# Rotary attention and a sigmoid-gated MLP in one kernel: weights decoded in fewer bit operations, and keys rotated together with queries

## The chip, the cores and the metric

The program runs on one core of one Trainium2 chip. Its engines are TensorE (PE, with its weight loads as PEld), VectorE (DVE), ScalarE (ACT) and GpSimd (POOL); SyncE (SP) issues the transfers. The metric is device microseconds of one execution; three runs of the kernel before have a median of 735.48 us (735.28 to 738.73).

## The reference

Four batches of eight heads, 576 positions, head size 64. Keys and queries are rotated (rotary embedding), attention is a softmax over 576 keys, and its output goes through a gated MLP (512 to 1536 to 512). The three MLP weights reach the kernel as 64-bit floats.

```python
def rotate(x):
    x1, x2 = (x[..., :half], x[..., half:])
    return np.concatenate([x1 * cos - x2 * sin, x1 * sin + x2 * cos], axis=-1)
scores = np.matmul(rotate(q), rotate(k).transpose(0, 1, 3, 2)) / np.sqrt(64)
attn = softmax(scores)
x = np.matmul(attn, v)             # (4, 8, 576, 64) -> (2304, 512)
out = (sigmoid(x @ w_gate) * (x @ w_val)) @ w_out
```

## The kernel before

**Order.** The program is written as tasks with a rank, a modelled cost, and tokens that they read and write. `Plan.order()` is a list scheduler: it takes the costs and ranks and gives each engine one fixed order, which is then emitted. SP's transfers are tasks in it too. So a changed cost moves instructions on every engine, and each engine and SP's queue run strictly in the order emitted.

**Work.** A batch's attention runs over four head pairs and two halves of the queries (256 and 320 columns). A half of a pair is two or three query blocks (128, 128, and a last one of 64 rows for both heads). Per block and head: scores on PE (line 470 for the first two batches, in f32), a scaled copy with row minimum on DVE (505), Exp on ACT (510), sum and reciprocal on DVE (513, 515), a scaled f16 copy on ACT (275) and its remainder on DVE (281). SP then transposes the block into `pt` (537); for the 64-row block it first moves the second head's rows next to the first's (`p<-p`, 534). The product with the values is on PE (547, tile `pv`), evicted into `xt` by ACT (275) and DVE (281). After the four pairs of a half, a small chain finds a scale: DVE reductions (556, 562), PE (252), DVE (254), PE (257), DVE (239 to 243, tile `c_s`). The MLP follows per half: `m<-xt,w` on PE (598), tanh on ACT (604), gating on DVE (608), split on ACT and DVE (275, 281, tile `gt`), then `m<-wo,gt` on PE (632).

**Weights.** `w_in_chunk` handles 12 chunks of 1024 numbers per partition for gate and value, `w_out_decode` 12 chunks of 512 for the output. Each 64-bit number is two words, `hi` and `lo`. ACT takes the sign from `hi` (286, tanh into int8) and prepares `lo` (291); DVE makes the 32-bit number in three operations (295, 298, 302). Then ACT takes the largest magnitude (324; 354 for `w_out`), PE spreads it (264), and ACT and DVE split the number into two f16 parts (275, 281, tile `w`). Chunks of `w_in` are staged in three slots; those of `w_out` in two, so the transfer of chunk n (348) waits for the DVE operation that last reads chunk n-2.

**Rotation.** `keys_queries` loads keys and queries of a pair side by side (411, x) and the same with swapped halves (412, y, tile `sw`, two buffers). For batches 0 and 1 DVE makes x*cos, y*sin and their sum for keys and for queries apart: six operations of 576 columns (416, 418, 420). For batches 2 and 3 POOL does the same.

Of the kernel before, what the change touches and what calls it, by code (L numbers as in the profile page):

```python
# [10 lines left out]
F32 = mybir.dt.float32  # L11
# [14 lines left out]
TINY = 2.0 ** -100  # L26


W_STEP = 0.5493 / 1.2 * 2.0 ** 15
NW = 2  # L30
TERMS = ((0, 0), (1, 0), (0, 1))
HALVES = ((0, 256), (256, 320))
# [124 lines left out]
def rope_attention_then_sigmoid_glu(ctx: ExitStack, tc: tile.TileContext, qk, v, w_in, w_out, tables, out):  # L157
# [57 lines left out]
    def op(e, us, rank, reads, writes, fn, port=False):  # L215
        P.add(((e, us),), rank, reads, writes, lambda _: fn(eng.get(e)), port=port)

    def op2(us, rank, reads, writes, fn):
        op("DVE", us, rank, reads, writes, fn, port=True)
# [61 lines left out]
        V.scalar_tensor_tensor(out=o, in0=src, scalar=scale, in1=hi, op0=ALU.mult, op1=ALU.subtract)  # L281


    def signs(o, hi):

        A.activation(o, hi.bitcast(F32), AF.Tanh, scale=W_STEP)

    def low_bits(lo):

        w = lo.bitcast(U32)  # L290
        A.activation(w, w, AF.Copy, scale=2.0 ** -29 * (1 - 2.0 ** -12), bias=2.0 ** -9 - 2.0 ** -13 - 0.5)

    def bits_1(o, hi):

        V.tensor_scalar(out=o, in0=hi, scalar1=3, scalar2=0x40000000, op0=ALU.logical_shift_left, op1=ALU.bitwise_xor)  # L295

    def bits_2(o, lo):
        V.scalar_tensor_tensor(out=o, in0=o, scalar=0x7FFFFFFF, in1=lo, op0=ALU.bitwise_and, op1=ALU.bitwise_or)  # L298

    def bits_3(o, sg):  # L300
        r = o.bitcast(F32)
        V.scalar_tensor_tensor(out=r, in0=r, scalar=3e38, in1=sg, op0=ALU.min, op1=ALU.mult)  # L302

    stage = [wo16[:, 4 * n:4 * n + 4].rearrange("p f a c -> p (f a c)").bitcast(I32).rearrange(
        "p (n w) -> p n w", w=2) for n in range(3)]
# [1 line left out]
    def w_in_chunk(f, rank):  # L307
        slot = ring("stage", 3)
        tok = [("wo", 4 * slot + n) for n in range(4)]
        t = stage[slot]  # L310
        hi, lo = t[:, :, 1], t[:, :, 0]
        dst = w16[:, f].rearrange("p g a c n -> p g a (c n)")
        sg = w16[:, f, 1].rearrange("p a c n -> p (a c n)").bitcast(I8)[:, 1024:2048]
        W = ("w", f)
        dma(rank - 0.15, [], tok, 1024, lambda: Y.dma_start(out=t.rearrange("p n w -> p (n w)"), in_=w_in[f].bitcast(I32)))
        op("ACT", c_act(1024), rank, tok, [W], lambda E: signs(sg, hi))
        op("ACT", c_act(1024), rank, [], tok, lambda E: low_bits(lo))
        op2(0.7, rank, [W], tok, lambda E: bits_1(hi, hi))
        op2(c_dve(1024, two=True), rank, [], tok, lambda E: bits_2(hi, lo))
        op2(c_dve(1024, two=True), rank, [W], tok, lambda E: bits_3(hi, sg))  # L320
        r = hi.bitcast(F32).rearrange("p (g n) -> p g n", g=2)
        M = ("wm", f)
        for g in range(2):
            op("ACT", c_act(512) + 0.2, rank, tok, [M, W], lambda E, g=g: A.activation(
                dst[:, g, 0], r[:, g], AF.Abs, accum_out=w_m[:, f, g:g + 1]))
        place = m_place()
        top = allsum(rank, w_m[:, f], 2, place, [M])
        pow2(rank, top, w_s[:, f], w_i[:, f], 14, [place[1]], [("ws", f)])
        for g in range(2):
            op("ACT", c_act(512), rank, tok + [("ws", f)], [W], lambda E, g=g: scaled(  # L330
                A, dst[:, g, 0], r[:, g], w_s[:, f, g:g + 1]))
# [9 lines left out]
    def w_out_decode(f, rank):  # L341
        o, tok = wo_slot(f)
        n = f % 2
        X = ("tmp", n)
        XT = [("xt", 1, p, i) for p in (0, 1) for i in range(2)] if n == 0 else [("xt", 1, p, i) for p in (2, 3) for i in range(2)]
        words = tmp[n][:, 0:1024].rearrange("p (n w) -> p n w", w=2)
        hi, lo, sg = words[:, :, 1], words[:, :, 0], tmp[n][:, 1024:1152].bitcast(I8)
        dma(rank - 0.05, [], [X] + XT, 512, lambda: Y.dma_start(out=tmp[n][:, 0:1024], in_=w_out[f].bitcast(I32)))
        op("ACT", c_act(512), rank, [], [X], lambda E: signs(sg, hi))
        op("ACT", c_act(512), rank, [], [X], lambda E: low_bits(lo))  # L350
        op2(0.4, rank, [X], [tok], lambda E: bits_1(o, hi))
        op2(c_dve(512, two=True), rank, [X], [tok], lambda E: bits_2(o, lo))
        op2(c_dve(512, two=True), rank, [X] + XT, [tok], lambda E: bits_3(o, sg))
        op("ACT", c_act(512) + 0.2, rank, [tok], ["sink", "wob"], lambda E: A.activation(
            sink[:, 0:512], o.bitcast(F32), AF.Abs, accum_out=wo_b[:, f:f + 1]))

# [42 lines left out]
    def keys_queries(b, p, rank):  # L399
# [365 lines left out]
```

## Time and profile before

| | |
|---|---|
| median of 3 runs | 735.48 us |
| span of the profiled execution | 733.1 us (the runs' median lies 2.4 us above it) |
| PE busy | 632.3 us, 86% |
| DVE busy | 526.3 us, 72% |
| ACT busy | 462.8 us, 63% |
| POOL busy | 74.8 us, 10% |
| chain that ended last, by engine | PE 73%, DVE 18%, DMA 4% |

Views used below. The page's slices: 40 equal parts of the span (18.3 us each), a digit is the busy share in tenths. The table by stretches: from:to, length, then busy us (and instructions) of PE, PEld, DVE, ACT and POOL, the granted TensorE clock (1.00 is full), the DMA engines' share, GB/s. The groups: line, engine, operation, out<-in, shape, count | busy us, mean ns of one | idle time of the engine just before and what ended it. The chain: start, length in us, what. The timeline: start, length, engine, line, operation.

### The profile page before, as it was taken

Reading aid. Unit: us, or ns where it says so; the run is one execution under the profiler, and the core shown is the slowest. Engines: PE = TensorE matmul, PEld = TensorE weight load, DVE = VectorE, ACT = ScalarE, POOL = GpSimd, SP = SyncE. Lnnn points to the kernel's source line nnn. Section 1 sums busy time; section 2 is a strip of 40 time slices with the busy share of each in tenths; the row PEclk is TensorE's granted clock in tenths of the full one; section 3 lists DMA queues with packets and bytes.
Section 4 is the critical chain, followed back from the end, with each engine's and each line's share of the span. In section 5 each row is a group of like instructions: output and inputs, shape, how many; then the busy total and the mean of one; then the engine's idle time right before and its main releaser. Section 6 shows DMA issues by size and latency. Waiting matters only on the chain.

```text
span 733.1 us, 12435 instructions
## 1 busy us (share of the span) xinstructions
PE 632.3 (86%) x4642; PEld 414.7 (57%) x4642; DVE 526.3 (72%) x1194; ACT 462.8 (63%) x940; POOL 74.8 (10%) x54
## 2 busy tenths in 40 slices
PE   2355885873279999999999999999999999999997
PEld 1133573551146754577657765578667756866753
DVE  6998899988988973688879998688948574421320
ACT  3767899886556984577758768676757564322320
POOL 0400000000031100014313130131300000000000
PEclk9976697786589999999999999999999999999999
DMA  9965744746934174389596779966483534000001
GB/s 365 318 140 148 233 130 165 198 128 175 255 106 130 34 176 113 86 175 190 130 199 140 160 147 195 202 149 138 105 187 90 118 70 115 1 2 29 1 9 35
DMA packets 187484, 100.55 MB, mean 137 GB/s; under 512 B 171040, under 2 KB 176288, under 8 KB 185376
## 3 DMA queue, kind: packets, MB, share of 16 engines
q1 hardware_dynamic: 187424, 99.77, 54.4%
q8 instruction: 36, 0.59, 0.3%
q14 instruction: 24, 0.20, 0.1%
HBM read 43.12 MB, written 4.72 MB: 65 GB/s over the span
## 4 chain that ended last, share of the span: by engine, by line
PE 73%; DVE 18%; DMA 4%; issue 2%; ACT 2%; SPq 0%; DVEq 0%; ACTq 0%
PE m L598 34%; PE m L632 19%; PE pv L547 9%; PE s L470 5%; PE s L482 5%; DVE p L281 3%; DMA pt<-p 3%; DVE p L505 2%; DVE wo L298 2%; DVE wo L302 2%; DVE sw L418 1%; DVE stk L420 1%; DVE w L281 1%; DMA sw<-in_qk_dram 1%; DVE wo L295 1%
## 5 line engine op out<-in xcount | busy, mean ns | idle before, releaser
L598 PE MATMUL m<-xt,w 128*128 128x320 f16 (+1 forms) x2304 | 303.6, 290 | 8.0 <-ACT w L275 2.6
L598 PEld LDWEIGHTS <-w 128*128 128x128 f16 x2304 | 224.9, 99 | 79.2 <-issue 14.9
L632 PE MATMUL m<-wo,gt 128*128 128x512 f16 x648 | 145.9, 380 | 0.0
L510 ACT ACTIVATE p<-p,st 128x576 f32<-128x576 f32 x144 | 110.6, 769 | 51.8 <-DVE p L505 43.4
L281 DVE SCALAR_TENSOR_TENSOR p<-p,st,p 128x576 f16<-128x576 f32 x144 | 117.2, 845 | 21.9 <-ACT p L275 21.3
L470 PE MATMUL s<-stk 64*128 64x288 f32 (+1 forms) x320 | 70.0, 508 | 52.7 <-DVE p L505 38.2
L275 ACT ACTIVATE p<-p,st 128x576 f16<-128x576 f32 x144 | 104.3, 764 | 14.6 <-DVE st L515 3.5
L632 PEld LDWEIGHTS <-gt 128*128 128x128 f16 x648 | 62.1, 98 | 73.1 <-issue 4.0
L547 PE MATMUL pv<-pt,v 128*64 128x256 f16 (+3 forms) x960 | 77.1, 312 | 21.5 <-DMA pt<-p 21.5
L608 DVE SCALAR_TENSOR_TENSOR th<-th,m 128x256 f32<-128x256 f32 (+1 forms) x96 | 43.1, 450 | 67.7 <-PE m L598 66.1
L275 ACT ACTIVATE gt<-th,c_s 128x256 f16<-128x256 f32 (+1 forms) x96 | 50.3, 528 | 50.0 <-DVE th L608 49.5
L547 PEld LDWEIGHTS <-v 128*64 128x64 f16 (+1 forms) x960 | 54.1, 118 | 44.7 <-issue 29.1
L470 PEld LDWEIGHTS s<-stk 64*128 64x128 f32 (+1 forms) x320 | 35.4, 210 | 76.6 <-DVE p L505 47.5
L604 ACT ACTIVATE th<-m,gsc 128x256 f32<-128x256 f32 (+1 forms) x96 | 47.1, 493 | 36.6 <-PE m L598 35.4
L281 DVE SCALAR_TENSOR_TENSOR gt<-th,c_s,gt 128x256 f16<-128x256 f32 (+1 forms) x96 | 53.4, 562 | 19.1 <-ACT gt L275 19.0
L505 DVE TENSOR_SCALAR_CACHE_REDUCE p<-s,q_e 128x576 f32<-128x576 f32 x72 | 57.5, 812 | 10.6 <-PE s L482 10.0
L505 DVE TENSOR_SCALAR_CACHE_REDUCE p<-s 128x576 f32<-128x576 f32 x72 | 53.4, 751 | 15.0 <-PE s L470 14.5
L418 POOL TENSOR_TENSOR sw<-sw,tab 128x576 f32<-128x576 f32 x16 | 25.4, 1590 | 264.7 <-DVE xm L556 174.1
L482 PE MATMUL s<-stk 128*128 128x288 f16 (+1 forms) x320 | 44.4, 288 | 0.4 <-DVE p L505 0.4
L416 POOL TENSOR_TENSOR qk<-qk,tab 128x576 f32<-128x576 f32 x16 | 25.1, 1593 | 181.0 <-DMA qk<-in_qk_dram 137.5
L275 ACT ACTIVATE o<-m,o_s 128x512 f32<-128x512 f32 x16 | 11.0, 685 | 42.2 <-PE m L632 42.0
L482 PEld LDWEIGHTS <-stk 128*128 128x128 f16 (+1 forms) x320 | 27.4, 100 | 13.9 <-issue 5.4
(94 smaller groups left out, 508.8 us busy)
## 6 DMA issues: line engine op xcount, KB each, us to landing
wo<-in_w_dram SPq DMA_DIRECT2D x12, 1024.0 KB, 5.6
sw<-in_qk_dram SPq DMA_DIRECT2D x16, 576.0 KB, 5.1
xt<-in_wo_dram SPq DMA_DIRECT2D x12, 512.0 KB, 4.4
stk<-in_qk_dram SPq DMA_DIRECT2D x8, 576.0 KB, 4.5
xt<-in_v_dram SPq DMA_DIRECT2D x4, 1152.0 KB, 6.6
qk<-in_qk_dram SPq DMA_DIRECT2D x8, 576.0 KB, 6.0
out_dram<-o SPq DMA_DIRECT2D x16, 256.0 KB, 2.2
stk<-sw SPq DMA_DIRECT2D x16, 216.0 KB, 3.6
```

The costliest lines, as they stand in the source:

```text
L275: A.activation(o, src, AF.Copy, scale=scale)
L281: V.scalar_tensor_tensor(out=o, in0=src, scalar=scale, in1=hi, op0=ALU.mult, op1=ALU.subtract)
L418: either(places, rank, gate, [Z[m]], lambda E, m=m: E.tensor_tensor(out=y[:, m], in0=y[:, m], in1=tab[:, 1], op=ALU.mult))
L470: T.matmul(s_ps[to[e]][hs if width == 64 else slice(0, 128), c, 0:288], lhsT=qT[hs, rows:rows + width], rhs=kT[hs, c * 288:c * 288 + 288], ...
L482: T.matmul(o[:, c, 0:288], lhsT=q[:, rows:rows + width], rhs=kk[:, c * 288:c * 288 + 288], start=(m == 0), stop=(m == 1))
L505: lambda E, h=h, c=c: V.tensor_scalar(out=p32[prs[c]].rearrange("p (c n) -> p c n", c=2), in0=s_ps[h][:, :, 0:288], scalar1=down, scalar2= ...
L510: lambda E, c=c: A.activation(p32[prs[c]], p32[prs[c]], AF.Exp, bias=st[:, k, 0, c:c + 1], scale=-1.0, accum_out=st[:, k, 1, c:c + 1]))
L547: T.matmul(v_ps[64 * e:64 * e + 64, 0:n], lhsT=v16[hs, p, a, g, :], rhs=pt[z][hs, c * 9 + g, 0:n], start=(first and m == 0), stop=(last an ...
L598: T.matmul(m_ps[m][:, 0:n], lhsT=w16[:, f, g, a, cc, :], rhs=x[:, cc, c, c0:c0 + n], start=(k == 0), stop=(k == 11))
L604: op("ACT", c_act(n), rank - 0.05, [("m", m), ("gsc", b, f)], [("th", r)], lambda E, m=m: A.activation(t, m_ps[m][:, 0:n], AF.Tanh, scale= ...
L608: op("DVE", c_dve(n, psum=True), rank - 0.05, [("m", m)], [("th", r)], lambda E, m=m: V.scalar_tensor_tensor(out=t, in0=t, scalar=1.0, in1 ...
L632: T.matmul(m_ps[m], lhsT=gt[:, f, a, c0:c0 + 128], rhs=wo16[:, f, c, :], start=(f == 0 and k == 0), stop=(f == NF - 1 and k == 2))
```

## The change

The weight decode: ACT now multiplies `hi`, read as a 32-bit float, by a power of two in place (a correction of the exponent) instead of taking its sign through tanh into a buffer of its own, and DVE builds the number in two operations, `magnitude` and `signed`, instead of three. The rotation for batches 0 and 1: x*cos, y*sin and the sum are each one operation over keys and queries together (1152 columns; the table is broadcast over the two).

```diff
-    def signs(o, hi):
-        A.activation(o, hi.bitcast(F32), AF.Tanh, scale=W_STEP)
+    def exponents(hi):
+        w = hi.bitcast(F32)
+        A.activation(w, w, AF.Copy, scale=2.0 ** -112)
...
-    def bits_1(o, hi):
-        V.tensor_scalar(out=o, in0=hi, scalar1=3, scalar2=0x40000000, op0=ALU.logical_shift_left, op1=ALU.bitwise_xor)
-    def bits_2(o, lo):
-        V.scalar_tensor_tensor(out=o, in0=o, scalar=0x7FFFFFFF, in1=lo, op0=ALU.bitwise_and, op1=ALU.bitwise_or)
-    def bits_3(o, sg):
-        r = o.bitcast(F32)
-        V.scalar_tensor_tensor(out=r, in0=r, scalar=3e38, in1=sg, op0=ALU.min, op1=ALU.mult)
+    def magnitude(o, hi, lo):
+        V.scalar_tensor_tensor(out=o, in0=hi, scalar=3, in1=lo, op0=ALU.logical_shift_left, op1=ALU.bitwise_or)
+    def signed(o, hi, m):
+        V.scalar_tensor_tensor(out=o, in0=hi, scalar=-2 ** 31, in1=m, op0=ALU.bitwise_and, op1=ALU.bitwise_or)
...
-        op("ACT", c_act(1024), rank, tok, [W], lambda E: signs(sg, hi))
+        op("ACT", c_act(1024), rank, [], tok, lambda E: exponents(hi))
         op("ACT", c_act(1024), rank, [], tok, lambda E: low_bits(lo))
-        op2(0.7, rank, [W], tok, lambda E: bits_1(hi, hi))
-        op2(c_dve(1024, two=True), rank, [], tok, lambda E: bits_2(hi, lo))
-        op2(c_dve(1024, two=True), rank, [W], tok, lambda E: bits_3(hi, sg))
+        op2(c_dve(1024, two=True), rank, [], tok, lambda E: magnitude(lo, hi, lo))
+        op2(c_dve(1024, two=True), rank, [], tok, lambda E: signed(hi, hi, lo))
...
+        if b < NW:
+            XX = X[0] + X[1]
+            cos, sin = (tab[:, n:n + 1].to_broadcast([128, 2, S]) for n in range(2))
+            op2(c_dve(2 * S, two=True), rank, gate, XX, lambda E: E.tensor_tensor(out=x, in0=x, in1=cos, op=ALU.mult))
+            op2(c_dve(2 * S, two=True), rank, gate, Z, lambda E: E.tensor_tensor(out=y, in0=y, in1=sin, op=ALU.mult))
+            op2(c_dve(2 * S, two=True), rank, Z, XX, lambda E: E.tensor_tensor(out=x, in0=x, in1=y, op=ALU.add))
+            slots[b, p] = p, None, -1.0 / D ** 0.5
+            return
```

`w_out_decode` changes as `w_in_chunk` does, at 512 columns. Since the scheduler sees fewer and cheaper DVE tasks, it also emits another order; in the new kernel `magnitude` and `signed` stand at lines 295 and 298, the rotation at 410 to 412, and what stood at 254, 281, 505, 537, 534, 348, 411, 412 and 562 now stands at 253, 280, 503, 535, 532, 342, 404, 405 and 560.

DVE, around the remainder of the last 64-row block of batch 0 (before at line 281, after at 280, both `p_82<-p_80,st,p_82`; `p` are the softmax blocks, `wo_62` a `w_out` chunk's target, `xt_65` its staged words, `sw_76` and `sw_77` the swapped keys and queries). Before:

```order
L281 SCALAR_TENSOR_TENSOR p_81<-p_79,st,p_81 128x576
L420 TENSOR_TENSOR stk<-stk,sw_76 128x576
L295 TENSOR_SCALAR wo_62<-xt_65 128x512
L298 SCALAR_TENSOR_TENSOR wo_62<-wo_62,xt_65 128x512
L302 SCALAR_TENSOR_TENSOR wo_62<-wo_62,xt_65 128x512
L416 TENSOR_TENSOR stk<-stk,tab 128x576
L281 SCALAR_TENSOR_TENSOR p_82<-p_80,st,p_82 128x576
```

After:

```order
L280 SCALAR_TENSOR_TENSOR p_81<-p_79,st,p_81 128x576
L410 TENSOR_TENSOR stk<-stk,tab 128x1152
L280 SCALAR_TENSOR_TENSOR xt_64<-pv,xt_64 128x320
L554 TENSOR_REDUCE xm<-xt_64 128x1
L295 SCALAR_TENSOR_TENSOR wo_62<-xt_65 128x512
L298 SCALAR_TENSOR_TENSOR wo_62<-xt_65,wo_62 128x512
L411 TENSOR_TENSOR sw_76<-sw_76,tab 128x1152
L412 TENSOR_TENSOR stk<-stk,sw_76 128x1152
L295 SCALAR_TENSOR_TENSOR wo_62<-xt_65 128x512
L298 SCALAR_TENSOR_TENSOR wo_62<-xt_65,wo_62 128x512
L280 SCALAR_TENSOR_TENSOR p_82<-p_80,st,p_82 128x576
```

Between the remainder of the block before (`p_81`) and that of the last block stand now two `w_out` chunks and a whole rotation of batch 1 instead of one chunk and two of its half operations.

SP's queue at the same place: the transpose of the block before (`p_81`), then the move and the transpose of the last block (`p_82`), among loads of `w_out` words (`xt_65`) and swapped keys and queries (`sw`). Before:

```order
L412 DMA sw_76<-in_qk_dram 128x1152
L537 DMA_TRANSPOSE pt_72<-p_81 128x18x128
L348 DMA xt_65<-in_wo_dram 128x1024
L534 DMA p_82<-p_82 64x2x576
L348 DMA xt_65<-in_wo_dram 128x1024
L412 DMA sw_77<-in_qk_dram 128x1152
L537 DMA_TRANSPOSE pt_72<-p_82 128x18x64
```

After:

```order
L342 DMA xt_65<-in_wo_dram 128x1024
L405 DMA sw_76<-in_qk_dram 128x1152
L535 DMA_TRANSPOSE pt_72<-p_81 128x18x128
L342 DMA xt_65<-in_wo_dram 128x1024
L532 DMA p_82<-p_82 64x2x576
L535 DMA_TRANSPOSE pt_72<-p_82 128x18x64
```

The two loads that stood between the move and the last transpose are gone from there; the load of `sw_76`, which waits for the DVE sum that last reads that buffer (before at 420, after at 412), stands ahead of the first of the two transposes in both.

DVE between the reduction over the four pairs of that half (562, after 560) and the row maximum that PE waits for (254, after 253). Before:

```order
L562 TENSOR_REDUCE xm<-xm 128x1
L295 TENSOR_SCALAR wo_62<-xt_65 128x512
L298 SCALAR_TENSOR_TENSOR wo_62<-wo_62,xt_65 128x512
L302 SCALAR_TENSOR_TENSOR wo_62<-wo_62,xt_65 128x512
L418 TENSOR_TENSOR sw_77<-sw_77,tab 128x576
L254 TENSOR_REDUCE row<-pv 1x1
```

After:

```order
L560 TENSOR_REDUCE xm<-xm 128x1
L295 SCALAR_TENSOR_TENSOR o_87<-xt_65 128x512
L298 SCALAR_TENSOR_TENSOR o_87<-xt_65,o_87 128x512
L511 TENSOR_SCALAR st<-st 128x2
L513 RECIPROCAL st<-st 128x2
L253 TENSOR_REDUCE row<-pv 1x1
```

Four operations of 512 or 576 columns became two, with two small ones behind them.

## Rows read from the trace of the kernel before

**Rows 1.** The page: busy time by engine, and slices of PE.

```profile
PE 632.3 (86%) x4642; PEld 414.7 (57%) x4642; DVE 526.3 (72%) x1194; ACT 462.8 (63%) x940; POOL 74.8 (10%) x54
...
PE   2355885873279999999999999999999999999997
```

**Rows 2.** Table by stretches, whole span.

```profile
0.00:90.00 90.00, 45.08 (x224) 27.11 (x224) 75.57 (x146) 58.44 (x115) 7.90 (x10) 0.83 0.78 240
90.00:188.00 98.00, 65.81 (x468) 45.40 (x466) 89.62 (x200) 83.69 (x172) 0.00 (x0) 0.81 0.58 163
188.00:217.00 29.00, 12.64 (x81) 8.02 (x82) 26.49 (x43) 13.60 (x29) 7.01 (x4) 0.66 0.70 196
217.00:300.00 83.00, 82.44 (x578) 48.72 (x576) 58.55 (x139) 57.10 (x119) 5.91 (x4) 1.00 0.43 103
300.00:733.00 433.00, 426.37 (x3298) 285.50 (x3296) 276.08 (x671) 249.94 (x508) 53.99 (x36) 1.00 0.51 112
```

**Rows 3.** Chain that ended last, from 186 to 232 us.

```profile
187.75 0.67 DVE stk L420
...
190.94 0.73 DVE p L281
...
195.06 4.89 DMA p<-p
199.97 3.92 DMA pt<-p
203.93 4.26 PE pv L547 x28
...
209.60 0.16 DVE xm L562
...
215.59 0.21 DVE row L254
```

**Rows 4.** Groups of DVE by shape, whole span.

```profile
L281 DVE SCALAR_TENSOR_TENSOR p<-p,st,p 128x576 f16<-128x576 f32 x144 | 117.2, 845 | 21.9 <-ACT p L275 21.3
...
L298 DVE SCALAR_TENSOR_TENSOR wo<-wo 128x1024 int32<-128x1024 int32 x12 | 15.7, 1312 | 0.6
...
L298 DVE SCALAR_TENSOR_TENSOR wo<-wo,xt 128x512 int32<-128x512 int32 x11 | 8.6, 786 | 0.8
L295 DVE TENSOR_SCALAR wo<-wo 128x1024 int32<-128x1024 int32 x12 | 8.3, 689 | 0.0
...
L295 DVE TENSOR_SCALAR wo<-xt 128x512 int32<-128x512 int32 x11 | 4.6, 418 | 0.0
```

**Rows 5.** Timeline of DVE from 8 to 16 us: one pair's rotation.

```profile
10.95 1.42 DVE L416 TENSOR_TENSOR stk<-stk,tab 128x576 f32<-128x576 f32 x2
...
14.53 0.76 DVE L420 TENSOR_TENSOR stk<-stk,sw 128x576 f32<-128x576 f32 x1
15.21 0.75 DVE L505 TENSOR_SCALAR_CACHE_REDUCE p<-s 128x576 f32<-128x576 f32 x1
```

**Rows 6.** Groups of ACT by shape, whole span.

```profile
L324 ACT ACTIVATE w<-wo 128x512 f16<-128x512 f32 x24 | 15.7, 659 | 5.2 <-DVE wo L302 5.2
L291 ACT ACTIVATE wo<-wo 128x1024 uint32<-128x1024 uint32 x12 | 13.5, 1128 | 0.0
L286 ACT ACTIVATE w<-wo 128x1024 int8<-128x1024 f32 x12 | 13.3, 1111 | 0.0
```

**Rows 7.** Waits of PE, 0 to 92 us: total, times, longest.

```profile
PE m L264 <- ACT w L324: 3.0, 2, 2.7
```

**Rows 8.** Timeline of SP's queue from 184 to 206 us.

```profile
185.58 2.02 SPq L537 DMA_TRANSPOSE pt<-p  x1
...
188.82 5.51 SPq L537 DMA_TRANSPOSE pt<-p  x1
```

**Rows 9.** Table by stretches, the last block of batch 0's attention.

```profile
188.00:210.00 22.00, 8.36 (x52) 5.38 (x53) 19.63 (x35) 10.10 (x22) 0.31 (x1) 0.55 0.92 259
```

**Rows 10.** Timeline of DVE and POOL from 209 to 217.5 us.

```profile
209.69 1.67 POOL L418 TENSOR_TENSOR sw<-sw,tab 128x576 f32<-128x576 f32 x1 [174.14 <-DVE xm L556]
...
210.19 1.72 DVE L298 SCALAR_TENSOR_TENSOR wo<-wo,xt 128x512 int32<-128x512 int32 x1
```

More of the change, by code (lines that the diff above doesn't have):

```diff
@@ L26 @@
 TINY = 2.0 ** -100
-W_STEP = 0.5493 / 1.2 * 2.0 ** 15
 NW = 2
@@ L312, in w_in_chunk @@
         dst = w16[:, f].rearrange("p g a c n -> p g a (c n)")
-        sg = w16[:, f, 1].rearrange("p a c n -> p (a c n)").bitcast(I8)[:, 1024:2048]
         W = ("w", f)
         dma(rank - 0.15, [], tok, 1024, lambda: Y.dma_start(out=t.rearrange("p n w -> p (n w)"), in_=w_in[f].bitcast(I32)))
-        op("ACT", c_act(1024), rank, tok, [W], lambda E: signs(sg, hi))
+        op("ACT", c_act(1024), rank, [], tok, lambda E: exponents(hi))
         op("ACT", c_act(1024), rank, [], tok, lambda E: low_bits(lo))
-        op2(0.7, rank, [W], tok, lambda E: bits_1(hi, hi))
-        op2(c_dve(1024, two=True), rank, [], tok, lambda E: bits_2(hi, lo))
-        op2(c_dve(1024, two=True), rank, [W], tok, lambda E: bits_3(hi, sg))
+        op2(c_dve(1024, two=True), rank, [], tok, lambda E: magnitude(lo, hi, lo))
+        op2(c_dve(1024, two=True), rank, [], tok, lambda E: signed(hi, hi, lo))
         r = hi.bitcast(F32).rearrange("p (g n) -> p g n", g=2)
@@ L346, in w_out_decode @@
         words = tmp[n][:, 0:1024].rearrange("p (n w) -> p n w", w=2)
-        hi, lo, sg = words[:, :, 1], words[:, :, 0], tmp[n][:, 1024:1152].bitcast(I8)
+        hi, lo = words[:, :, 1], words[:, :, 0]
         dma(rank - 0.05, [], [X] + XT, 512, lambda: Y.dma_start(out=tmp[n][:, 0:1024], in_=w_out[f].bitcast(I32)))
-        op("ACT", c_act(512), rank, [], [X], lambda E: signs(sg, hi))
+        op("ACT", c_act(512), rank, [], [X], lambda E: exponents(hi))
         op("ACT", c_act(512), rank, [], [X], lambda E: low_bits(lo))
-        op2(0.4, rank, [X], [tok], lambda E: bits_1(o, hi))
-        op2(c_dve(512, two=True), rank, [X], [tok], lambda E: bits_2(o, lo))
-        op2(c_dve(512, two=True), rank, [X] + XT, [tok], lambda E: bits_3(o, sg))
+        op2(c_dve(512, two=True), rank, [X], [tok], lambda E: magnitude(o, hi, lo))
+        op2(c_dve(512, two=True), rank, [X] + XT, [tok], lambda E: signed(o, hi, o))
         op("ACT", c_act(512) + 0.2, rank, [tok], ["sink", "wob"], lambda E: A.activation(
@@ L413, in keys_queries @@
         gate = ["tab"] + ([("ws", 8 + p)] if b == 1 else [])
-        places = [("POOL", c_pool(S, two=True))] if b > 1 else [("DVE", c_dve(S, two=True))]
+        if b < NW:
[6 more added lines that the diff above has]
+            return
+        places = [("POOL", c_pool(S, two=True))]
         for m in range(2):
@@ L421, in keys_queries @@
                 out=x[:, m], in0=x[:, m], in1=y[:, m], op=ALU.add))
-        if b < NW:
-            slots[b, p] = p, None, -1.0 / D ** 0.5
-            return
         X = X[0] + X[1]
```

## The prediction

> **What bounds the kernel now.** I read the page first: PE is busy 632.3 of 733.1 us, and its slices are full only from the thirteenth on [rows 1]. The table by stretches says where the change-over lies [rows 2]: up to 217 us PE is busy 45.08 + 65.81 + 12.64 = 123.5 us and idle for 93.5, and DVE is busy 75.57 + 89.62 + 26.49 = 191.7 us, 88%; from 217 us on PE is busy 82.44 of 83 and 426.37 of 433 us at full clock. So the kernel is a DVE-led first part of 217 us and a PE-bound second part of 516 us. The work of PE does not change. What the edit is worth is how much earlier the second part can start, and whatever DVE saves behind that point is covered by PE.
>
> The start of the second part hangs on the end of batch 0's attention. In the chain [rows 3] the last rotation sum before it is at 187.75, the last block's remainder ends at 190.94 + 0.73 = 191.7, the move of its rows starts only at 195.06 and takes 4.89, its transpose 3.92, the product with the values 4.26, the reduction over the pairs comes at 209.60, the row maximum at 215.59, and from 217 us on PE is full [rows 2].
>
> **The change, part by part.**
>
> *One DVE operation less per chunk.* Twelve of 689 ns and twelve of 418 ns go [rows 4]: 8.3 + 5.0 = 13.3 us busy. Two operations in a row overlap: two of 0.75 take 1.42 [rows 5], 0.08 less. So 24 x 0.08 = 1.9 us of it was never on the clock, and 11.4 us remain. The two operations that stay are taken at the price of the old second one, 1312 and 786 ns [rows 4]; both are two-input operations of the same shape.
>
> *ACT's operation* reads and writes `hi` in place, as its neighbour does with `lo`: 1128 against 1111 ns [rows 6], so at most 12 x 0.017 = 0.2 us more. I cost it at nothing.
>
> *Rotation.* One pair takes 15.21 - 10.95 = 4.26 us for six operations [rows 5]. No row shows 1152 columns. From 512 to 1024 columns the price rises by (1312 - 786)/512 = 1.03 ns a column [rows 4], so 1152 cost 0.76 + 576 x 0.00103 = 1.35 us, three of them less two overlaps 3.9 to 4.0. I take 0.3 us a pair, 8 x 0.3 = 2.4 us in all. Bounds: 0 (if each is two old ones) and 24 x (0.76 - 0.59) = 4.0 us (if the whole fixed part of each dropped operation is saved).
>
> [...]
>
> DVE so loses 11.4 + 2.4 = 13.8 us, all of it in the first part. If that were the whole story the second part would start 13.8 us earlier. It is not, because the scheduler fills the room. Counted in the two orders, ahead of the reduction over batch 0's second half stand now 40 instead of 38 score copies, 38 instead of 36 remainders, 11 instead of 10 `w_out` chunks, and all of batch 1's rotation instead of all but five of its half operations. At 0.75 [rows 5] and 0.845 [rows 4], 2 x 0.786 for the chunk and 0.68 for a half operation that is 1.5 + 1.7 + 1.6 + 3.4 = 8.2, less overlap about 7 us of work pulled ahead of the point that counts. DVE's own saving there is then 13.8 - 7 = 6.8 us. The path through that point, stage by stage:
>
> (a) *First half of batch 0, to about 90 us.* DVE has the same work as before there (one decoded chunk more in place of what was dropped), so no gain. ACT has more: seven chunk decodes instead of five, 12 instead of 8 magnitudes and two more scaled copies, 2 x (1.111 + 1.128) + 4 x 0.66 + 2 x 0.66 = 8.4 us [rows 6], about 9 with the reads of four sums. It has room: 58.44 busy of 90 [rows 2]. But PE's order is fixed, and its sums over the magnitudes already wait 3.0 us for ACT in this part [rows 7]; behind them stand score and value products. I take +1 us; bounds 0 and +9.
>
> (b) *From there to the second-to-last transpose.* It stands in SP's queue behind the load that waits for a rotation sum (before the one at 187.75 [rows 3]). Counted in the two orders, DVE decodes from the first half's reduction to that sum six `w_in` chunks instead of seven (6 x 2.62 = 15.7 instead of 7 x 3.31 = 23.2 us), eight `w_out` chunks instead of six (12.6 instead of 11.9), makes nine whole rotation operations instead of six half ones (9 x 1.27 = 11.4 instead of 4.1), two splits and a score copy less (-2.3): -7.5 + 0.7 + 7.3 - 2.3 = -1.8. DVE is busy 89.62 of 98 us there [rows 2]: -2 us. Bounds 0 and -5 (if ACT's earlier chunks also take idle out of this stretch).
>
> (c) *The last block.* From that transpose's issue at 188.82 [rows 8] to the reduction at 209.60 [rows 3] are 20.8 us, of which SP held the queue 5.51 us with one transpose [rows 8] while the block's remainder had been ready since 191.7. The two loads that stood behind the move are gone from there, and the last transpose follows it directly. That is the gain; against it, the DMA engines are 92% busy there [rows 9], and one load of `w_out` and one of `sw` more than before (1.1 MB, 4 us at 259 GB/s) now stand ahead of the last transpose. I take -1 us; bounds +4 (those loads) and -5 (a transpose issue of 2.02, as the one before had [rows 8], and a quicker move).
>
> (d) *Reduction to row maximum*, 209.60 to 215.59 [rows 3]: 6.0 us for four operations that run beside POOL at 1.72 us each instead of 0.79 [rows 4, 10]. Two of the four are gone, and two small ones come in: -2 us; bounds 0 and -3.
>
> **Sum:** +1 - 2 - 1 - 2 = -4 us. Behind that point nothing is gained: PE covers DVE, whose remaining work shrinks by the 7 us pulled ahead. 733.1 - 4 = 729.1 us of span; the median of the runs lies 2.4 us above the span, so **731.5 us**. Half a per cent (3.7 us) is about what a measurement can tell from no change.
>
> **Rivals.**
>
> 1. *DVE's whole saving is carried.* If the stretches before 217 us are DVE-bound throughout, as 88% busy suggests, and the pulled work sits in idle time, the start moves by nearly all of 13.8 us: 735.5 - 12 = 723.5. Against it: the last 20.8 us hang on SP and transfers, not on DVE. Chance 0.15.
>
> 2. *No gain: the end of batch 0's attention is set by transfers.* The loads are the same, the DMA engines are 92% busy from 188 to 210 us [rows 9], and the last transposes waited for the queue, not for DVE. Earlier DVE work only asks for the same loads sooner; what (b) and (d) save comes back as longer issues in (c). Then 733.5 to 737, say 735.5. Against it: DMA is busy only 0.58 of the stretch before [rows 2], so loads asked for sooner have room there. Chance 0.25.
>
> 3. *Slower: ACT in the first half.* If the two chunk decodes pulled ahead find no idle ACT, PE's in-order sums hold the value products behind them and the first half ends up to 9 us later. The rest recovers what (b) to (d) give, 5 us, only if DVE is then the later one; with ACT late it recovers 2 to 3. The result is 735.5 + 9 - 3 = 741.5. It decides from about 8 us of ACT waiting in front of the magnitude sums, on top of the 3.0 there now. Against it: 31 us of idle ACT in that stretch [rows 2], though some of it is before the first data arrive. Chance 0.11.
>
> That the change does not do what it says is hardly a case: the two operations per chunk stand in the emitted order.
>
> **How the numbers follow.** The forecast has 0.49. Its bounds, from all lower ends (0 - 5 - 5 - 3 = -13, unlikely together) to +3 when two terms fail, spread it over both sides of 731.8; I give some three quarters of it to faster. Faster: 0.37 + 0.15 = 0.52. Same: 0.12 + 0.25 = 0.37. Slower: 0.11. The range takes in the likely part of rival 1 and all of rival 2: 722 to 738, with about 0.1 left above and 0.08 below.
>
> **What would show it.** The group of the old first operation is gone with its 24 instructions, and DVE's busy time falls by 13.3 us and up to 5 more for the rotation. A rotation operation at 1152 columns lasts 1.30 to 1.40 us. PE's unbroken run starts at 209 to 214 us instead of 216, and the stretch behind it is as full as before. In (a) the half's reduction comes at 88 to 93 us; in (c) the transpose issue ahead of the move is shorter than 5.51 us; in (d) the row maximum follows the reduction by about 4 us. The forecast is wrong if PE starts before 206 or after 217 us, or if PE's busy time itself moves by more than 3 us.

## The result, and the profile after

The changed kernel has a median of 724.49 us (four runs, 724.20 to 726.02), against 735.38 us for the kernel before (four runs, 733.84 to 738.73): 10.9 us less by the medians. The ratio, estimated from the single runs and so not quite the quotient of the medians, is 0.9866 with a 95% interval of 0.9827 to 0.9905. The profiled execution took 724.2 us with a span of 722.4, so 10.7 us of span went.

Part 1 and the first line of part 2 of the page of the changed kernel, as in [rows 1] for before:

```profile
span 722.4 us, 12369 instructions
PE 635.5 (88%) x4642; PEld 417.3 (58%) x4642; DVE 511.1 (71%) x1146; ACT 463.1 (64%) x940; POOL 74.3 (10%) x54
PE   2446696765399999999999999999999999999997
```

DVE is 15.2 us less busy, with 48 instructions fewer. PE's slices are full from the twelfth on and not from the thirteenth. Where that comes from is seen in the table by stretches, which answers to [rows 2]:

```profile
0.00:90.00 90.00, 45.51 (x214) 27.02 (x214) 75.30 (x137) 65.28 (x126) 8.98 (x10) 0.90 0.83 257
90.00:188.00 98.00, 67.96 (x492) 48.31 (x490) 92.51 (x193) 84.94 (x176) 0.00 (x0) 0.81 0.69 183
188.00:217.00 29.00, 22.89 (x137) 13.82 (x135) 22.02 (x49) 16.45 (x37) 12.14 (x8) 0.70 0.73 159
217.00:300.00 83.00, 83.00 (x584) 48.91 (x584) 50.06 (x123) 53.37 (x110) 0.00 (x0) 1.00 0.37 89
300.00:722.00 422.00, 416.13 (x3226) 279.23 (x3222) 271.17 (x645) 243.06 (x495) 53.17 (x36) 1.00 0.50 113
```

The third row is the one to read: PE is busy 22.89 of the 29 us from 188 to 217, where it was 12.64 before [rows 2], at nearly the same granted clock (0.70 and 0.66). POOL is in that row too, with 12.14 us, and DVE is not less busy in the row before it: 92.51 against 89.62 us.

The chain of waits of the changed kernel around the last block (start, length, what), against [rows 3]:

```profile
184.45 6.22 SPq L535
191.39 4.48 DMA p<-p
195.89 3.56 DMA pt<-p
199.50 4.35 PE pv L545 x17
```

Everything in it stands 4 us earlier, and the issue of the transpose ahead of the move is no shorter: 6.22 us against 5.51 [rows 8]. The end of the block, in the timelines of POOL and of DVE, against [rows 10]:

```profile
195.03 1.80 POOL L421 TENSOR_TENSOR qk<-qk,sw 128x576 f32<-128x576 f32 x1
207.50 1.40 POOL L419 TENSOR_TENSOR sw<-sw,tab 128x576 f32<-128x576 f32 x1 [10.67 <-DMA sw<-in_qk_dram]
```

```profile
205.28 0.16 DVE L560 TENSOR_REDUCE xm<-xm 128x1 f32<-128x4 f32 x1
205.35 0.68 DVE L295 SCALAR_TENSOR_TENSOR o<-xt 128x512 int32<-128x512 int32 x1
206.06 0.69 DVE L298 SCALAR_TENSOR_TENSOR o<-xt,o 128x512 int32<-128x512 int32 x1
206.95 0.26 DVE L253 TENSOR_REDUCE row<-pv 1x1 f32<-1x128 f32 x1
```

From the reduction over the pairs to the row maximum pass 1.7 us and not 6.0. POOL's rotations of batch 2 now run before and after this gap and not in it, so a bit operation takes 0.69 us here and not 1.72 [rows 10].

PE now runs without a gap from the product with the values at 199.50 us on; before, it still waited 2.7 us for the row maximum and ran on from 215.84. One line of the table by stretches for the changed kernel:

```profile
199.50:240.00 40.50, 40.50 (x303) 27.00 (x303) 34.92 (x80) 31.40 (x64) 6.09 (x4) 0.93 0.42 97
```

**One table for all kernels.** The prediction cut the path into stages: (a) to the reduction over the first half of batch 0; (b) from there to the issue of the second-to-last transpose; (c) from that issue to the reduction over the second half; (d) from there to the row maximum; then the rest. These are the starts of the named instructions in the profiled executions, subtracted, in us. Each profile is one execution, and executions of one kernel differ by several us: 25 of the kernel before, taken beside runs 1 to 4, lie between 732.0 and 738.9 us. So a difference of a microsecond or two between lines means little. The medians are over all runs. The first two lines are the kernels compared, the others the experiments that follow. Run 6 is not in it, since its profile shows the two transposes as one piece.

| kernel | (a) | (b) | (c) | (d) | rest | span | median |
|---|---|---|---|---|---|---|---|
| before | 90.1 | 98.8 | 20.8 | 5.9 | 517.6 | 733.1 | 735.4 |
| changed | 92.1 | 92.3 | 20.8 | 1.7 | 515.4 | 722.4 | 724.5 |
| 1: new work, old order | 90.8 | 98.9 | 20.5 | 5.1 | 517.8 | 733.0 | 731.1 |
| 2: old work, new order | 100.1 | 100.6 | 20.0 | 2.1 | 514.6 | 737.4 | 740.2 |
| 3: decode alone | 97.5 | 98.5 | 18.9 | 1.4 | 515.3 | 731.6 | 734.2 |
| 4: rotation alone | 88.0 | 105.2 | 21.9 | 1.9 | 516.5 | 733.5 | 734.1 |
| 5: transpose before one load | 93.3 | 91.8 | 20.7 | 1.7 | 515.9 | 723.3 | 723.6 |
| 7: as 1, half sums | 88.6 | 98.9 | 20.5 | 5.0 | 517.8 | 730.7 | 730.6 |
| 8: changed, half sums | 93.3 | 92.4 | 22.1 | 1.7 | 514.6 | 724.1 | 725.1 |
| 9: before, HOP 0.24 | 92.7 | 94.7 | 22.0 | 2.2 | 519.6 | 731.2 | 728.4 |
| 10: changed, HOP 0.24 | 92.9 | 92.7 | 20.6 | 2.7 | 514.5 | 723.3 | 724.9 |
| 11: changed, HOP 0.21 | 93.0 | 89.0 | 20.6 | 2.1 | 518.9 | 723.6 | 728.5 |
| 12: before, HOP 0.21 | 94.1 | 94.2 | 22.4 | 1.9 | 525.0 | 737.6 | 739.4 |

(c) is 19 to 22 us whatever is done. (d) is 5 to 6 us in the order of before and 1.4 to 2.7 in every other order, whether an operation was dropped or not. What differs is (b), and partly (a). The rest is 514.5 to 517.8 us, but 518.9 to 525.0 in runs 9, 11 and 12.

### The profile page after: what moved, and what is told of

Its sections match the earlier page's. It is cut to its first block, busy times and chain, and to the rows that moved or that the text cites. A ratio compares the mean times of both kernels' runs of the same rounds, so it can differ in the third digit from the quotient of the medians.

```text
span 722.4 us, 12369 instructions
## 1 busy us (share of the span) xinstructions
PE 635.5 (88%) x4642; PEld 417.3 (58%) x4642; DVE 511.1 (71%) x1146; ACT 463.1 (64%) x940; POOL 74.3 (10%) x54
## 4 chain that ended last, share of the span: by engine, by line
PE 74%; DVE 15%; DMA 3%; ACT 3%; issue 3%; SPq 1%; ACTq 0%; DVEq 0%
PE m L596 35%; PE m L630 20%; PE pv L545 8%; PE s L480 5%; PE s L468 4%; DVE p L280 3%; DVE p L503 2%; DMA pt<-p 2%; DVE wo L295 2%; DVE wo L298 1%; DVE w L280 1%; DVE sw L411 1%; SPq L535 1%; DVE v L280 1%; DVE stk L412 1%
## 5 line engine op out<-in xcount | busy, mean ns | idle before, releaser
L596 PE MATMUL m<-xt,w 128*128 128x320 f16 (+1 forms) x2304 | 299.8, 288 | 7.5 <-ACT th L602 6.6
L280 DVE SCALAR_TENSOR_TENSOR p<-p,st,p 128x576 f16<-128x576 f32 x144 | 119.8, 862 | 24.2 <-ACT p L274 23.6
L468 PE MATMUL s<-stk 64*128 64x288 f32 (+1 forms) x320 | 76.1, 528 | 56.1 <-DVE p L503 46.0
L274 ACT ACTIVATE p<-p,st 128x576 f16<-128x576 f32 x144 | 104.4, 764 | 15.7 <-DMA pt<-p 5.6
L468 PEld LDWEIGHTS s<-stk 64*128 64x128 f32 (+1 forms) x320 | 38.5, 216 | 82.3 <-DVE p L503 58.4
L545 PEld LDWEIGHTS <-v 128*64 128x64 f16 (+1 forms) x960 | 54.2, 119 | 31.9 <-issue 20.5
L280 DVE SCALAR_TENSOR_TENSOR gt<-th,c_s,gt 128x256 f16<-128x256 f32 (+1 forms) x96 | 54.8, 576 | 20.5 <-ACT gt L274 20.4
L274 ACT ACTIVATE o<-m,o_s 128x512 f32<-128x512 f32 x16 | 10.9, 682 | 42.0 <-PE m L630 42.0
```

The lines of the kernel that those rows point to most:

```text
L274: A.activation(o, src, AF.Copy, scale=scale)
L468: T.matmul(s_ps[to[e]][hs if width == 64 else slice(0, 128), c, 0:288], lhsT=qT[hs, rows:rows + width], rhs=kT[hs, c * 288:c * 288 + 288], ...
L545: T.matmul(v_ps[64 * e:64 * e + 64, 0:n], lhsT=v16[hs, p, a, g, :], rhs=pt[z][hs, c * 9 + g, 0:n], start=(first and m == 0), stop=(last an ...
L596: T.matmul(m_ps[m][:, 0:n], lhsT=w16[:, f, g, a, cc, :], rhs=x[:, cc, c, c0:c0 + n], start=(k == 0), stop=(k == 11))
```

## The experiments

### Is it the work or the order?

The scheduler gives the new costs a new order, so two things changed at once. Runs 1 and 2 take them apart; runs 3 and 4 make half of the change each, planned anew.

**Run 1, the new work in the old order.** The tasks of before stay in the plan with their costs; the dropped ones emit nothing.

```diff
-        op2(0.7, rank, [W], tok, lambda E: bits_1(hi, hi))
-        op2(c_dve(1024, two=True), rank, [], tok, lambda E: bits_2(hi, lo))
-        op2(c_dve(1024, two=True), rank, [W], tok, lambda E: bits_3(hi, sg))
+        op2(0.7, rank, [W], tok, lambda E: None)
+        op2(c_dve(1024, two=True), rank, [], tok, lambda E: magnitude(lo, hi, lo))
+        op2(c_dve(1024, two=True), rank, [W], tok, lambda E: signed(hi, hi, lo))
...
```

> The work of the changed kernel in the order of the kernel before: two VectorE operations per chunk and whole rotation operations, each standing where the old ones stood; the places of the dropped ones stay empty. Theory W (the gain is VectorE's work, which runs without a gap in the stretch before the last transposes): VectorE's busy time falls by some 15 us, the stretch from 92 us to the release of the second-to-last transpose shrinks by 5 us or more, and the time is 724 to 728 us. Theory O (the gain is the order that the planner makes of it: loads and POOL's rotations earlier, fewer operations between the last reduction and the row maximum): with the old order POOL still runs beside the row maximum and the gap there stays 4 to 6 us; the time is 731 to 735 us. Theory T (transfers set the last block): the release comes earlier, but the issue ahead of the move grows by as much, 733 to 736 us.

Measured: 731.09 us (ten runs, 728.90 to 734.79, the profiled one the longest), ratio 0.9961 (0.9942 to 0.9980). That is 3.4 us less, at the lower edge of theory O's range (731 to 735), and its gap of 4 to 6 us is there: 5.1 in (d).

**Run 2, the old work in the new order.** Two of the three old operations, or the two halves of a rotation, are emitted in the place of one.

```diff
-        op2(c_dve(1024, two=True), rank, [], tok, lambda E: magnitude(lo, hi, lo))
-        op2(c_dve(1024, two=True), rank, [], tok, lambda E: signed(hi, hi, lo))
+        op2(c_dve(1024, two=True), rank, [], tok, lambda E: (bits_1(hi, hi), bits_2(hi, lo)))
+        op2(c_dve(1024, two=True), rank, [], tok, lambda E: bits_3(hi, sg))
...
```

> The work of the kernel before (three VectorE operations per chunk, signs by tanh, half rotation operations) in the order of the changed kernel; the extra operation follows directly behind its neighbour. Theory W: nothing of the gain is left, 734 to 740 us, since the new order has more work ahead of the point that counts. Theory O: the row maximum follows the last reduction within 2 to 3 us as in the changed kernel, POOL is out of that gap, and 727 to 731 us are reached with the old work. Theory T: 733 to 737 us.

Measured: 740.22 us (four runs), ratio 1.0088 (1.0059 to 1.0116). That is just above theory W's range (734 to 740). Of theory O the short gap came true, 2.1 us in (d), but not the time.

So neither theory holds alone. The same work is worth 735.4 - 731.1, about 4 us (3.4 by the pair measured together), in the old order, and 740.2 - 724.5 = 15.7 us in the new one. The order alone, with the old work, costs 5 to 6 us. The tables by stretches, cut at the milestones (the first half's reduction, the release of the transpose, the row maximum), show part of why. Here stage (b) alone, first in the old order (before, then run 1), then in the new (run 2, then the changed kernel); the columns are PE, PEld, DVE, ACT, POOL:

```profile
90.05:188.42 98.37, 65.75 (x468) 45.40 (x466) 90.03 (x200) 84.04 (x172) 0.00 (x0) 0.80 0.58 164
```

```profile
90.77:189.20 98.43, 64.86 (x468) 45.55 (x466) 83.71 (x184) 84.05 (x172) 0.00 (x0) 0.82 0.60 162
```

```profile
100.07:200.20 100.13, 64.36 (x476) 46.89 (x474) 95.58 (x204) 80.64 (x167) 0.00 (x0) 0.82 0.64 171
```

```profile
92.13:184.05 91.92, 64.66 (x478) 46.06 (x474) 87.45 (x181) 80.13 (x167) 0.00 (x0) 0.83 0.71 186
```

In the new order DVE is busy 95% of the stretch with either work, and 8.1 us less of it make the stretch 8.2 us shorter. That is half of the 15.7 us; the other half lies in (a), 100.1 us in run 2 and 92.1 in the changed kernel, with 5.2 us less of DVE's work (81.68 and 76.44 us busy). What makes up the rest there isn't shown. In the old order 6.3 us less of DVE's work leave (b) as long as it was, in the executions profiled. Run 1's profile is the longest of its ten and shows nothing of the 3.4 us, so some of them may belong here; run 7, with the same order, has 98.9 us in an execution 1.9 us above its median. The granted clock, 0.80 to 0.83 in the four tables, doesn't tell them apart. DVE was busy 92% there before, and yet it was not what set the end. The chain of waits tells what took its place. In before, DVE holds 63 of the 99 us of the chain in this stretch (37.3 up to 140 us, 25.9 behind) and ACT 0.6. In run 1 DVE holds 34 (19.8 and 14.5) and ACT 29 (22.2 and 6.4). Pieces of it in run 1 (start, length, what), none of which is in the chain of before:

```profile
113.32 1.32 ACT w L321 x4
115.03 1.01 ACT wo L287
116.94 1.41 ACT w L275 x2
118.75 1.05 ACT wo L287
122.22 1.31 ACT w L321 x4
```

It looks as if paths of nearly the same length lay beside each other, and as one was cut another took over.

**Run 3, the decode alone,** with the old six half operations of the rotation.

```diff
-        if b < NW:
-            XX = X[0] + X[1]
...
-        places = [("POOL", c_pool(S, two=True))]
+        places = [("POOL", c_pool(S, two=True))] if b > 1 else [("DVE", c_dve(S, two=True))]
...
```

> The new decode alone, the old half rotations, planned anew. Theory W: 13.3 us of the 15.2 us of VectorE's busy time go here, so most of the gain, 725 to 728 us. Theory O: it depends on the plan that comes out; the time goes with the place of POOL's rotation sums and not with VectorE's busy time, anywhere from 725 to 735 us. A theory R (the whole rotation is what lets the loads of batch 2 and POOL's operations come earlier) gives 731 to 735 us.

Measured: 734.18 us (ten runs), ratio 0.9986 (0.9963 to 1.0009). Theory W is wrong by its own number: 11.5 us of DVE's work are gone (busy 514.8 us), and no time.

**Run 4, the rotation alone,** with the three old bit operations.

```diff
-        op2(c_dve(1024, two=True), rank, [], tok, lambda E: magnitude(lo, hi, lo))
-        op2(c_dve(1024, two=True), rank, [], tok, lambda E: signed(hi, hi, lo))
+        op2(0.7, rank, [W], tok, lambda E: bits_1(hi, hi))
+        op2(c_dve(1024, two=True), rank, [], tok, lambda E: bits_2(hi, lo))
+        op2(c_dve(1024, two=True), rank, [W], tok, lambda E: bits_3(hi, sg))
...
```

> The whole rotation operations alone, the old decode, planned anew. Theory W: 2 to 2.4 us of VectorE's work, so 732.5 to 735 us. Theory R (the rotation is what counts): 726 to 730 us. Theory O: by the plan, and then the row maximum follows the last reduction by 2 us and not by 6.

Measured: 734.14 us (ten runs), ratio 0.9999 (0.9985 to 1.0012): in theory W's range, with theory O's short gap, and against theory R. In both runs (d) fell to 1.4 and 1.9 us, 4 us that were won there; they were lost in (a) for run 3 (97.5 us) and in (b) for run 4 (105.2). Two halves that give nothing each give 10.9 us together: what each is worth depends on the order that the planner makes of it.

### Does SP's queue set the last block?

In the changed kernel the second-to-last transpose stands in SP's queue behind two loads, one of which waits 1.6 us for a rotation sum; its own rows were ready 6.7 us before. Runs 5 and 6 move the transpose ahead of one load and of both. Nothing else moves on any engine. Run 5 swaps the last two of these three, run 6 moves the transpose past both; SP's order in run 6, against the changed kernel's:

```
- 59 DMA xt_65<-in_wo_dram 128x1024
- 60 DMA sw_76<-in_qk_dram 128x1152
- 61 DMA_TRANSPOSE pt_72<-p_81 128x18x128
+ 59 DMA_TRANSPOSE pt_72<-p_81 128x18x128
+ 60 DMA xt_65<-in_wo_dram 128x1024
+ 61 DMA sw_76<-in_qk_dram 128x1152
```

> The changed kernel with two neighbours on SP swapped and nothing else: the second-to-last transpose of batch 0 (issued at 184.45 us, 6.22 long) goes ahead of the load of batch 2 that waits for the rotation sum ending at 184.04. Its rows were ready at 177.7. Theory Q (the queue sets the last block: waiting load ahead, transpose issue lengthened by the load's traffic): the transpose is issued at about 182.5, takes 2 to 3.5 us, the move follows at 187 to 188 and not at 191.4, and the time falls by 3 to 5 us, to 719.5 to 721.5. Theory T (the transfers in flight set it, whatever the order): the transpose takes as long, only the 2 us of waiting are won, and they are lost again where the load, now later, makes POOL run beside the row maximum: 723 to 725. Against both: if DVE's order is what the move waits for, no change, 724 to 725.

Measured: 723.64 us (six runs, 721.75 to 725.07), ratio 0.9850 (0.9821 to 0.9880), which can't be told from the changed kernel's and is in theory T's range. The transpose was not issued earlier after all, at 185.05 us and not at 182.5, since the one before it came later (180.28 us) and held the queue for 4.09 us. Its own issue was shorter, 4.47 us and not 6.22, and (c) stayed at 20.7 us.

> As the run before, and the chunk load that stood before that load (issued at 181.92) goes behind the transpose too. Theory Q: the transpose is issued right behind its predecessor at about 181.9, takes 2 us or so, 718.5 to 721. But the chunk's bytes come 2 to 3 us later, and ScalarE's decode of that chunk stands ahead of exponentials of batch 1: if that hurts, 1 to 2 us more than the run before. Theory T: 723 to 725.

Measured: 725.34 us (six runs), ratio 0.9873 (0.9840 to 0.9906): 0.3 us above theory T's range and far from theory Q's. SP's timeline in run 6:

```profile
179.50 5.78 SPq L546 DMA_TRANSPOSE pt<-p  x2
187.22 0.62 SPq L541 DMA_DIRECT2D p<-p  x1
193.75 1.30 SPq L546 DMA_TRANSPOSE pt<-p  x1
```

The two transposes are through the queue at 185.3, as theory Q wanted, and the move is issued at 187.22 where it was 191.39. But the last transpose, which waits for the move to land, comes 6.5 us behind it and not 4.5, and the product after it then waits for PE's own order: scores of batch 1 stand ahead of it and wait for DVE, 2.6 us up to 198.24. The reduction comes at 205.37 us, in the changed kernel at 205.28. What the queue gave, the transfers and PE's order took back.

### Is ScalarE what holds the old order?

In run 1 PE waits 9.6 us for ACT's magnitude sums in stage (b). Runs 7 and 8 halve these sums in both orders.

```diff
-            dst[:, g, 0], r[:, g], AF.Abs, accum_out=w_m[:, f, g:g + 1]))
+            dst[:, g, 0, 0:256], r[:, g, 0:256], AF.Abs, accum_out=w_m[:, f, g:g + 1]))
...
-            sink[:, 0:512], o.bitcast(F32), AF.Abs, accum_out=wo_b[:, f:f + 1]))
+            sink[:, 0:256], o.bitcast(F32)[:, 0:256], AF.Abs, accum_out=wo_b[:, f:f + 1]))
```

> The new work in the old order, with ScalarE's sums of magnitudes taken over half the columns only (256 of 512, in all 36 operations), so that the scales are no longer the reference's. It takes some 0.23 us x 36 = 8 us from ScalarE and nothing from VectorE. Theory A (in the old order ScalarE, not VectorE, holds the stretch from 92 to 189 us: TensorE waits 9.6 us for these very sums there): the time falls by 3 to 6 us against the new work in the old order (731.1), to 725 to 728. Theory L (a loop of latencies holds it, each engine waiting in turn): under 1.5 us, 729.5 to 731.

Measured: 730.55 us (eleven runs, 728.09 to 734.48), ratio 0.9948 (0.9923 to 0.9973); run 1 had 731.09. A twelfth execution took 2198.78 us and is left out; what happened in it is not known.

> The changed kernel with the same halved sums; the scales are not the reference's. Theory A: in the new order VectorE is the bound (busy 87.5 of 91.9 us between the two reductions' stretches), so ScalarE's 8 us are worth under 1.5 us: 723 to 725. If ScalarE binds both orders, 718 to 721.

Measured: 725.14 us (six runs), ratio 0.9871 (0.9841 to 0.9901). ACT's group in run 7, by form:

```profile
L321 ACT ACTIVATE w<-wo 128x256 f16<-128x256 f32 x24 | 10.1, 421 | 4.0 <-DVE wo L299 3.9
```

The sums took 421 ns where they took 659 [rows 6], so the work did go, and it bought nothing that can be measured in either order. (b) is 98.9 us in run 7 as in run 1, and 98.8 in before: in this order 6 us of DVE's work and 4.6 of ACT's (84.05 to 79.47 us busy) can go from it without the end coming earlier. Theory L holds as far as these runs reach: neither DVE nor ACT alone bounds the old order. The chain of waits of run 7 from 139 to 190 us is spread over PE (16.7 us), DVE (12.2), transfers (10.5) and ACT (6.3). Which loop of waits holds the 98.9 us stays open.

### How much of the gain is the plan?

If an order decides what a saving is worth, the order of before may itself have been a poor throw. The planner assumes a wait between engines, `HOP`, of 0.2 us. Runs 9 to 12 change that one number in both kernels; the instructions are the same, in another order. Runs 9 to 11 were measured on one chip and run 12 on another, each beside the kernel before on that chip (736.96 and 734.81 us).

```diff
-    HOP = 0.2
+    HOP = 0.24
```

> The kernel before with one number of its planner changed, the wait that it assumes between engines (HOP 0.24 instead of 0.2): the same instructions in another order. Theory G (the gain is carried by any order that is planned for the new work): within 2 us of the kernel before, 733 to 737. Theory C (each plan is a throw, and part of the measured gain is the chance of the two plans compared): anywhere within 5 us of it on either side, 729 to 740, and so the gain at this setting is not the one measured.

Measured: 728.35 us (four runs, 725.19 to 733.03; the profiled one is the longest), ratio 0.9860 (0.9793 to 0.9928) to the kernel before.

> The changed kernel with the same number changed. Theory G: 8 to 11 us under the kernel before at the same setting, 723 to 727. Theory C: a difference of anything from 0 to 14 us, as the two runs with half of the change each came out 10 us apart from the sum.

Measured: 724.91 us (four runs, 724.70 to 725.10), ratio 0.9828 (0.9775 to 0.9881) to the kernel before.

> The changed kernel with HOP 0.21. Theory G: 723 to 726. Theory C: 718 to 732; a plan with more room ahead of the last block could come out faster than the changed kernel.

Measured: 728.47 us (four runs), ratio 0.9870 (0.9811 to 0.9928).

> The kernel before with HOP 0.21: the partner of the changed kernel at that setting (728.5). Theory G: 733 to 737. Theory C: anywhere from 728 to 741; with the two pairs so far, 10.9 us apart at HOP 0.2 and 3.4 at HOP 0.24, the third pair should come out between 0 and 14 apart, and it is the mean of the three that tells what the change itself is worth.

Measured: 739.41 us (nine runs), ratio 1.0061 (1.0038 to 1.0084).

Theory C, and more than it allowed: run 9 lies 0.6 us below its range. Of theory G only the time of run 10 came true, and not its distance of 8 to 11 us. With all the old work in it, the kernel before at HOP 0.24 has 728.35 us: some 7 of the 10.9 us are to be had with no change of work (8.6 against the kernel before on the same chip). The three pairs are 10.9 us apart at 0.2, 10.9 at 0.21 (739.41 - 728.47) and 3.4 at 0.24, mean 8.4. By the ratios, each to the kernel before on its own chip, they are 9.9, 14.0 and 2.4 us apart. The change was faster in each, though at 0.24 the two intervals overlap. The three plans of the old work spread over 11 us, the three of the new work over 4.

At HOP 0.24 the row to look at is again the one from 188 to 217 us. Before at HOP 0.24, then the changed kernel at HOP 0.24:

```profile
188.00:217.00 29.00, 15.64 (x101) 10.14 (x102) 27.12 (x48) 15.66 (x34) 5.77 (x4) 0.65 0.66 188
```

```profile
188.00:217.00 29.00, 23.14 (x136) 14.47 (x137) 26.27 (x57) 19.07 (x42) 8.21 (x5) 0.71 0.86 205
```

PE is busy 12.64 us of this stretch in before [rows 2], 15.6 and 15.5 in the same work under the two other plans, and 22 to 23 in the changed work under all three. But the row does not decide alone. Run 12 reaches its row maximum at 212.64 us, 2.9 us ahead of before, and is 4 us slower all the same: PE then idles 12.9 us behind that point (525.0 long, 512.1 busy) and 7.6 in before. So "PE covers DVE" behind the row maximum, which the prediction took for granted, also depends on the plan.

None of these versions beats the changed kernel by more than the measurement can tell; run 5 comes nearest, 0.9 us lower by the medians.

## Why the prediction was right, and where it was not

The forecast was 731.5 us in a range of 722 to 738, faster by more than half a per cent at 0.52. 724.5 lies in the range, and faster was the likelier side. The gain was forecast at 4 us and measured at 10.9: the time is in a range that was wide enough to take in the first rival, and the sum itself is 7 us off. By two of the signs that the prediction gave for itself, the forecast failed. PE runs without a gap from 199.5 us on, where 209 to 214 was forecast and anything before 206 was to count against it; and PE's busy time moved by 3.2 us (635.5 - 632.3), where more than 3 was to count. Terms (a) and (c) gave 2 us less than was taken, (b), (d) and what lies behind 9 us more; that their sum stayed inside the range is in part luck.

- **The price of the work: right in busy time.** DVE's busy time fell by 15.2 us, inside the 13.3 "and up to 5 more". The new groups by form:

```profile
L295 DVE SCALAR_TENSOR_TENSOR wo<-wo 128x1024 int32<-128x1024 int32 x12 | 15.8, 1320 | 0.0
L298 DVE SCALAR_TENSOR_TENSOR wo<-wo 128x1024 int32<-128x1024 int32 x12 | 15.2, 1266 | 0.2
L412 DVE TENSOR_TENSOR stk<-stk,sw 128x1152 f32<-128x1152 f32 x8 | 10.8, 1355 | 0.2
```

  A whole rotation operation takes 1355 ns; 1.35 us was interpolated. One pair's rotation takes 3.93 us where it took 4.26, so 0.33 us less a pair where 0.3 was taken. The bit operations were priced at 1312 and 786 ns and took 1320 and 1266, and 685 and 689 on 512 columns. Two operations of 0.75 against one of 1.35 save 0.15 us in length, and 1.42 against 1.35 only 0.07 on the clock [rows 5].

- **The price on the clock: mis-sized.** The prediction took 0.08 us off each dropped operation, since the two operations of [rows 5] overlap by that much. Those two do not need each other's result. The dropped operation was followed by the one that reads its result, and that one starts later. The timeline of DVE before:

```profile
199.84 0.42 DVE L295 TENSOR_SCALAR wo<-xt 128x512 int32<-128x512 int32 x1
200.36 0.69 DVE L298 SCALAR_TENSOR_TENSOR wo<-wo,xt 128x512 int32<-128x512 int32 x1
```

  Between the two lie 0.10 us. They are neighbours in at least 15 of the 24 places, with 0.10 or 0.11 us between them in 13 of these. An estimate from this is 13.3 + 15 x 0.10 - 9 x 0.08 = 14.1 us on DVE's clock, where the prediction had 11.4.

- **(a) +1 us: +2.1.** Inside its bounds of 0 to +9, and for the reason given: ACT is busy 65.28 us of the first 90 and not 58.44 [rows 2], and PE's waits for ACT's magnitudes rose from 3.0 us [rows 7] to 6.6:

```profile
PE m L263 <- ACT w L318: 6.6, 2, 5.8
```

- **(b) -2 us: -6.5, beyond its bound of -5.** This is the step that failed. The count of DVE's work was near: -1.8 forecast, 90.03 - 87.45 = 2.6 us measured. But the step then took the stretch to shrink by that work and no more. DVE's idle time in it fell too, from 98.37 - 90.03 = 8.3 to 91.92 - 87.45 = 4.5 us. The bound named this ("if ACT's earlier chunks also take idle out of this stretch") and allowed 3 us for it. ACT's busy time there did fall from 84.04 to 80.13 us, but runs 7 and 8 show that shorter ACT operations alone bring nothing. The idle time came out with the order: run 2, the old work in that order, has 100.13 - 95.58 = 4.5 us of it too. Which part of the order does it isn't shown.

- **(c) -1 us: 0.** The transpose's issue did not shorten (6.22 against 5.51 us), and runs 5 and 6 show that this would not have helped: in run 5 it did, to 4.47 us, and (c) stayed. Here the second rival, that transfers give back what is saved, was right.

- **(d) -2 us: -4.2, beyond its bound of -3, and for another reason.** The step took the gain from two operations dropped beside POOL. Runs 9 and 12 drop none and have 2.2 and 1.9 us; run 1 drops them and has 5.1. What counts is what the plan puts into the gap and where POOL runs. In the kernel before, the same bit operation (298) takes 0.69 us with POOL idle, as in the line at 200.36 above, and 1.72 us beside POOL [rows 10]. The two behind it there are as slow: 302 takes 1.78 us at 211.95 and 0.69 at 201.09 with POOL idle, 418 takes 1.95 us at 213.65 and 0.75 at 201.70. What holds them is not shown.

- **Behind that point: 0 forecast, 2.1 us measured** (517.6 to 515.4 in the table). PE idles 7.6 us in it before and 6.3 in the changed kernel, and is busy 0.8 us less. Its wait of 2.7 us for the row maximum lies ahead of this point but for 0.3 us, so that belongs to (d). The sum: +2.1 - 6.5 + 0 - 4.2 - 2.1 = -10.7, which is the 10.7 us of span.

- **The rivals.** The first rival's time, 723.5, was within 1 us, but its reason, a first part that is DVE-bound throughout, holds for (b) in the new order only: (c) did not move, and in the old order the same 15 us of DVE's work are worth 3.4. The third rival, ACT late in the first half, did not decide: (a) grew by 2.1 us.

What the prediction lacked was a way to see the order as a cause of its own. It counted how the order moved work past a point, 7 us of it, and took that as given back. In fact that same order lets DVE run at 95% of (b) instead of 92%.

## What to carry to other kernels

Where a list scheduler makes the order, an edit is two changes, fewer instructions and another plan, and each can be measured alone: emit the new work into the old order, and the old work into the new one. An engine that is busy 92% of a stretch need not be what bounds it; look whether the stretch shortens when its work goes, or whether the chain of waits just moves over to another engine. Before a gain of a per cent is put down to an edit, turn some neutral constant of the planner and see how far the time of unchanged work scatters: here it scattered by as much as the gain.

## What was not expected of the hardware

- The issue of one transpose on SP took from 1.28 us (run 11, at 193.90) to 6.56 us (run 8, at 185.69) around the last block. The three longest, 6.22 us in the changed kernel (at 184.45), 6.11 in run 4 (at 193.18) and that of run 8, each began 0.05 us behind the issue of a load. In run 6 the move was issued 4.2 us earlier (187.22 us and not 191.39), but the last transpose, which waits for it, came 6.5 us behind it and not 4.5, and the last block took 19 to 22 us in every order of the table.
- In one place an operation with one input was slow beside POOL too; [rows 10] shows it for one with two. The old first bit operation on 512 columns, 418 ns on average [rows 4], took 1.52 us in run 9. The timelines of DVE and of POOL there:

```profile
210.18 1.52 DVE L295 TENSOR_SCALAR wo<-xt 128x512 int32<-128x512 int32 x1
```

```profile
210.00 1.41 POOL L420 TENSOR_TENSOR qk<-qk,sw 128x576 f32<-128x576 f32 x1
```

  The operation starts inside POOL's and ends 0.3 us behind it: it looks as if it had been held until POOL's was over. In the kernel before, the same operation started 0.02 us ahead of POOL's (209.67 and 209.69 us) and took 0.42, so which of the two comes first may decide. Two pairs of rows do not settle it.
